# Transposing masked scores on TensorE in the first two chunks of an attention and feed-forward kernel

## The chip, the core and the metric

The kernel runs on one core of one Trainium2 chip, as one program with one launch. The metric is the device time of that program in microseconds. Five engines work side by side: TensorE (PE in the rows, its weight loads PEld), VectorE (DVE), ScalarE (ACT), GpSimd (POOL) and SyncE (SP), whose queue issues nearly all transfers.

## What is computed

The reference is sliding-window attention with four sink keys, followed by a two-layer feed-forward with an ELU between (B = 4, H = 8, S = 768, D = 64, 3072 tokens, d_model = 512, d_ff = 2048, all float32):

```
scores = q @ k.T / sqrt(D)
keep = (key < n_sink) | ((0 <= row - key) & (row - key < window))
scores = where(keep, scores, -1e9) - max
a = exp(scores);  a = a / (sum(a) + 1e-9)
x = a @ v                                  # heads side by side: 3072 x 512
h = x @ w_in;  g = h if h > 0 else exp(h) - 1
out = g @ w_out
```

## The kernel before

The 3072 tokens are cut into ten chunks of two or three tiles of 128 rows (`CHUNKS`). Chunks 0 and 1 take the first tile of each of the four sequences: there all keys of a query lie in one tile, so one 128x128 block of scores per head and tile is enough. They go through `attention_f32`, the others through `attention`. For each chunk attention is done for four pairs of heads (`NP`), and `feed_forward` follows: for each of 16 blocks of d_ff (`NF`), `stage1` forms h (line 867), ACT, DVE and POOL form ELU split into two float16 halves, and `stage2` adds g @ w_out into PSUM (line 897). The feed-forward of chunks 0 and 1 is cut in halves of eight blocks that alternate (`PARTS`), while the 32 pieces of the weights are still being loaded and converted. A piece goes from its load (`raw`) through an ACT step into the one PSUM bank (line 338), bit steps on POOL, ACT or DVE (lines 339 to 343), a DVE step (line 344), and two halves on ACT (line 503) and POOL (line 504).

In `attention_f32` one pair of heads goes through these steps:

- `scores` (line 593): queries times keys, query rows on partitions, two heads, for each of two tiles.
- line 600, DVE: one instruction scales by -0.125, adds the mask, writes the result to a tile `e` and takes its minimum along the row into `tops` (a second, short instruction reads the minimum out).
- `turned` (lines 607 to 610): the scores are computed a second time with keys on partitions (line 607), the mask is added by a matmul with an identity (line 609) and the row's minimum by another with eight times the identity (line 610).
- line 615, ACT: exp, out of PSUM into `pt`.
- `values` (line 631): values times `pt`, with the 64 columns of a head on partitions, and a matmul with a tile of ones which leaves the sum in every one of 64 rows.
- lines 640 to 645: the sum scaled (ACT or DVE), its reciprocal over 128x256 elements (DVE, line 641), the product (DVE, line 642), and two float16 halves (ACT, line 644; DVE or POOL, line 645). Their tile `x` is the input of `stage1`.

Chunk 0 alternates between two pairs of PSUM banks (`s` and `acc`) and three for the products; chunk 1 has one pair (`s`) and one bank (`last_end`).

The order of the work comes from a planner (`Plan`). Every step is a `Task` with an engine, a duration in the planner's terms, dependencies and ring buffers. The planner places the tasks, tries some 250 variations and keeps the best; `keep_order` then fixes the order of the instructions on each engine and of the transfers on SP. So a step that waits holds up all that stands behind it on its engine. `filled` puts matmuls that compute nothing (line 1242) in front of early PE tasks where the planner sees a gap. The first transfers stand ahead of the plan (line 1267).

Of the kernel before, what the change touches and what calls it, by code (L numbers as in the profile page):

```python
# [20 lines left out]
P = 128  # L21
# [29 lines left out]
TURNED = 2  # L51
# [9 lines left out]

KQ_OFF, V_OFF, KQ_COLS, V_COLS = {}, {}, 0, 0
for _c, _ch in enumerate(CHUNKS):
    for _p in range(NP):
        V_OFF[_c, _p] = V_COLS
        V_COLS += (len(key_tiles(_ch)) + 1) * P
        for _e in range(2):
            KQ_OFF[_c, 2 * _p + _e] = KQ_COLS
            if _c >= WHOLE or _e:
                KQ_COLS += len(key_tiles(_ch)) * KW + len(_ch) * P  # L70
# [9 lines left out]
class Task:  # L80
    __slots__ = ("eng", "dur", "lat", "fn", "args", "deps", "succ", "pos", "start", "due", "n", "ways", "done", "gap", "port", "mode", "turn")

    def __init__(self, eng, dur, fn, args, deps, lat, pos, gap, port, mode):
# [14 lines left out]
class Plan:  # L98
# [17 lines left out]
    def add(self, eng, dur, fn, *args, deps=(), lat=0.0, pos=None, or_=(), gap=2.0, port=None, mode=None):  # L116

        t = Task(eng, dur, fn, args, deps, lat, pos, gap, port, mode)
        for way in or_:
            t.ways[way[0]] = way[1:]  # L120
        self.tasks.append(t)
        return t
# [55 lines left out]
    def replay(self, dice=None):  # L178
# [7 lines left out]
        ready = dict.fromkeys(self.tasks, 0.0)  # L186
# [49 lines left out]
    def forward(self):  # L236
        left = {t: len(t.deps) for t in self.tasks}
        ready = {t: 0.0 for t in self.tasks}
# [156 lines left out]
def fast_path(tc, ctx, first, kq, vx, wt, out, nw, inside, flag, limits):  # L395
# [45 lines left out]
    ident8 = pool.tile([P, P], F16, name="ident8")  # L441
    ident16 = pool.tile([P, P], BF16, name="ident16")
    nc.scalar.activation(ident16, ident, AF.Copy)
    nc.scalar.activation(ident8, ident, AF.Copy, scale=8.0)
# [115 lines left out]
    def attention_f32(c):  # L560
# [6 lines left out]
        kw, vw = kc + qc, nt * P  # L567
# [3 lines left out]
        for p in range(NP):  # L571
# [14 lines left out]
            for j in range(nt):  # L586
# [8 lines left out]
                sc = add("PE", 0.25 if c or k > 2 else 0.55, scores, mode="rows", deps=[ldk], pos=at[k])  # L595
# [717 lines left out]
```

## Time and profile before

| what | us |
|---|---|
| median of 3 runs | 628.2 |
| lowest, highest | 626.99, 628.41 |
| the profiled execution, its own time | 628.24 |
| its span, first to last instruction | 626.2 |
| PE busy | 610.9 (98%) |
| DVE busy | 489.3 (78%) |
| ACT busy | 443.4 (71%) |
| POOL busy | 270.5 (43%) |

The span is 2.0 us shorter than the execution's own time. The busy shares are means over the whole span; PE's ends are modelled, so its busy time is an upper figure. The feed-forward lines 867 and 897 hold most of PE's time (1920 and 1200 matmuls).

### The profile page before, as it was taken

Reading aid. Unit: us, or ns where it says so; the run is one execution under the profiler, and the core shown is the slowest. Engines: PE = TensorE matmul, PEld = TensorE weight load, DVE = VectorE, ACT = ScalarE, POOL = GpSimd, SP = SyncE. Lnnn points to the kernel's source line nnn. Section 1 sums busy time; section 2 is a strip of 40 time slices with the busy share of each in tenths; the row PEclk is TensorE's granted clock in tenths of the full one; section 3 lists DMA queues with packets and bytes.
Section 4 is the critical chain, followed back from the end, with each engine's and each line's share of the span. In section 5 each row is a group of like instructions: output and inputs, shape, how many; then the busy total and the mean of one; then the engine's idle time right before and its main releaser. Section 6 shows DMA issues by size and latency. Waiting matters only on the chain.

```text
span 626.2 us, 14317 instructions
## 1 busy us (share of the span) xinstructions
PE 610.9 (98%) x4861; PEld 388.7 (62%) x4861; DVE 489.3 (78%) x1309; ACT 443.4 (71%) x1263; POOL 270.5 (43%) x531
## 2 busy tenths in 40 slices
PE   8899899999999999999999999999999999999997
PEld 6666566667776555667755556766455567765553
DVE  4988889999987567899997689998986899732222
ACT  2478999998887467699875578887765788733222
POOL 2557778555543343445342344433434445412221
PEclk9899999999999999999999999999999999999999
DMA  8467487779986455698974867987937688700001
GB/s 314 130 233 270 128 257 277 185 194 248 210 172 169 109 143 122 146 246 189 169 207 91 211 128 191 204 193 163 231 88 180 138 223 161 162 19 35 1 0 57
DMA packets 127427, 103.18 MB, mean 165 GB/s; under 512 B 96498, under 2 KB 102898, under 8 KB 127346
## 3 DMA queue, kind: packets, MB, share of 16 engines
q1 hardware_dynamic: 127200, 102.12, 65.9%
q8 instruction: 40, 0.66, 0.4%
q14 instruction: 41, 0.34, 0.2%
q10 hardware_dynamic: 146, 0.07, 0.0%
HBM read 71.75 MB, written 7.34 MB: 126 GB/s over the span
## 4 chain that ended last, share of the span: by engine, by line
PE 83%; DVE 6%; ACT 6%; issue 2%; DMA 1%; POOL 0%; SPq 0%; ACTq 0%; DVEq 0%; POOLq 0%
PE h L867 35%; PE acc L897 28%; PE last_acc L897 6%; PE s L756 2%; PE s L757 2%; PE last_end L827 2%; PE s L827 2%; DMA kqs<-in_kq_dram 1%; DVE rx L641 1%; ACT last_acc L338 1%; ACT w L503 1%; PE last_end L631 1%; ACT g L875 1%; DVE wv L344 1%; ACT gh L881 1%
## 5 line engine op out<-in xcount | busy, mean ns | idle before, releaser
L867 PE MATMUL h<-x,w 128*128 128x256 f16 (+1 forms) x1920 | 275.5, 294 | 3.7 <-DVE gl L883 1.5
L867 PEld LDWEIGHTS <-w 128*128 128x128 f16 x1920 | 187.0, 98 | 78.9 <-issue 5.0
L886 POOL TENSOR_TENSOR gl<-g,gh 128x256 f16<-128x256 f32 (+1 forms) x143 | 118.4, 829 | 189.2 <-ACT gh L881 145.9
L897 PE MATMUL acc<-w,gh 128*128 128x512 f16 x636 | 175.0, 379 | 0.0
L897 PEld LDWEIGHTS <-gh 128*128 128x128 f16 x792 | 74.7, 98 | 67.3 <-ACT gh L881 0.6
L875 ACT ACTIVATE g<-h 128x256 f32<-128x256 f32 (+1 forms) x160 | 67.1, 420 | 62.4 <-PE h L867 57.8
L881 ACT ACTIVATE gh<-g 128x256 f16<-128x256 f32 (+1 forms) x143 | 65.7, 460 | 50.0 <-DVE g L880 49.3
L897 PE MATMUL acc<-w,gl 128*128 128x512 f16 x318 | 96.9, 379 | 0.1
L781 ACT ACTIVATE e<-e,st 128x264 f32<-128x264 f32 x160 | 81.5, 510 | 18.2 <-DVE st L779 17.7
L794 DVE SCALAR_TENSOR_TENSOR pq<-e,st,pq 128x256 f16<-128x256 f32 x160 | 84.4, 548 | 7.9 <-ACT pq L793 7.4
L877 DVE TENSOR_SCALAR g<-g 128x256 f32<-128x256 f32 (+1 forms) x95 | 34.6, 364 | 71.1 <-ACT g L875 70.5
L793 ACT ACTIVATE pq<-e,st 128x256 f16<-128x256 f32 x160 | 75.4, 503 | 6.8 <-ACT g L875 3.2
L880 DVE SCALAR_TENSOR_TENSOR g<-g,h 128x256 f32<-128x256 f32 (+1 forms) x144 | 68.3, 475 | 6.5 <-ACT g L877 5.1
L779 DVE CUSTOM_DVE_ANT_0 e<-s,m 128x264 f32<-128x264 f32 x160 | 64.6, 426 | 6.4 <-PE s L757 5.7
L897 PEld LDWEIGHTS <-gl 128*128 128x128 f16 x396 | 38.1, 98 | 44.5 <-DVE gl L883 0.5
L682 ACT ACTIVATE kq<-kqs 128x912 f16<-128x912 f32 (+1 forms) x56 | 48.0, 862 | 8.5 <-PE s L757 5.4
L785 POOL TENSOR_SCALAR st<-st 128x2 f32<-128x2 f32 x80 | 21.5, 269 | 70.3 <-ACT e L781 60.0
L897 PE MATMUL last_acc<-w,gh 128*128 128x512 f16 (+1 forms) x126 | 45.3, 366 | 0.0
L504 POOL TENSOR_TENSOR w<-wv,w 128x512 f16<-128x512 f32 x32 | 39.0, 1226 | 13.8 <-ACT w L503 13.5
L685 DVE SCALAR_TENSOR_TENSOR kq<-kqs,kq 128x528 f16<-128x528 f32 (+1 forms) x56 | 38.0, 679 | 2.7 <-ACT kq L682 1.9
L756 PE MATMUL s<-kq 128*128 128x264 f16 x144 | 37.2, 276 | 0.2 <-DVE st L779 0.2
L757 PE MATMUL s<-kq 128*128 128x264 f16 x144 | 37.2, 276 | 0.0
(170 smaller groups left out, 837.9 us busy)
## 6 DMA issues: line engine op xcount, KB each, us to landing
raw<-in_wt_dram SPq DMA_DIRECT2D x32, 512.0 KB, 4.8
kqs<-in_kq_dram SPq DMA_DIRECT2D x32, 456.0 KB, 3.9
kqs<-in_kq_dram SPq DMA_DIRECT2D x28, 326.0 KB, 3.4
out_dram<-wv SPq DMA_DIRECT2D x21, 256.0 KB, 4.4
vs<-in_vx_dram SPq DMA_DIRECT2D x16, 320.0 KB, 4.2
qk<-in_kq_dram SPq DMA_DIRECT2D x24, 195.0 KB, 5.2
vs<-in_vx_dram SPq DMA_DIRECT2D x16, 256.0 KB, 3.3
qk<-in_kq_dram SPq DMA_DIRECT2D x24, 163.0 KB, 4.2
```

The lines of the kernel that those rows point to most:

```text
L756: nc.tensor.matmul(sp[:, :wd], q, hi[:, c0 : c0 + wd], start=True, stop=False)
L757: nc.tensor.matmul(sp[:, :wd], q, lo[:, c0 : c0 + wd], start=False, stop=True)
L779: red = add("DVE", 0.08 + 0.00104 * wd, lambda ee=ee, me=me, sp=sps[e], m=m, wd=wd: nc.vector.tensor_tensor_reduce(ee, sp[:, :wd], m[:, :w ...
L781: ex = add("ACT", act_us(wd, sums=True), lambda ee=ee, me=me, rs=rs[:, e : e + 1]: nc.scalar.activation(ee, ee, AF.Exp, bias=me, scale=-1. ...
L793: a = add("ACT", act_us(nb * P, True), lambda src=src, hi=hi, re=re: nc.scalar.activation(hi, src, AF.Copy, scale=re), deps=[rr])
L794: b = add("DVE", dve_us(nb * P) + 0.03, lambda src=src, hi=hi, lo=lo, re=re: nc.vector.scalar_tensor_tensor(lo, src, re, hi, ALU.mult, ALU ...
L867: nc.tensor.matmul(hp[:, :n], win[:, part, d, :], xx[:, :n], start=k == 0, stop=k == 3 * ND - 1)
L875: a = add("ACT", act_us(n) + 0.06, lambda gf=gf, hp=hp, sums=sums: nc.scalar.activation(gf, hp[:, :n], AF.Exp, scale=1.0 / G_SCALE, accum_ ...
L880: b = add("DVE", dve_us(n) - 0.035, lambda gf=gf, gd=gd, hp=hp: nc.vector.scalar_tensor_tensor(gd, gf, 0.0, hp[:, :n], ALU.min, ALU.max), ...
L881: th = add("ACT", act_us(n) - (0.03 if near else 0.0), lambda gd=gd, gh=gh: nc.scalar.activation(gh[:, :n], gd, AF.Copy), deps=[b])
L886: tl = add("POOL", pool_us(n), lambda gl=gl, gd=gd, gh=gh: nc.gpsimd.tensor_tensor(gl[:, :n], gd, gh[:, :n], ALU.subtract), deps=[th])
L897: nc.tensor.matmul(to[:, : cols.stop - cols.start], gg[:, i * P : (i + 1) * P], wout[:, part, cols], start=f == f0 and k == 0, stop=f == f ...
```

## The change

- In `attention_f32`, `turned` no longer computes the scores again. It transposes the masked scores `e` that DVE has written, in TensorE's transpose mode, two per task, and takes the minimum off by a matmul with minus the identity (`minus`). The matmul that added the mask is gone, and exp's scale becomes -1.
- `values` has `pt` as the stationary operand: queries are rows, and there are 65 columns for each head and tile. The 65th column of the values, which the layout of the input now carries, is a constant, so that the sum comes out beside the product. There are four matmuls in the place of eight.
- The sum's constant is added, and its reciprocal taken, on 128x4 elements, both on DVE. The product is formed with that column broadcast. A new step `upright` turns the product back by two TensorE transposes into the same bank; ACT and DVE make the float16 halves out of PSUM (POOL has no such step any more).
- The ring `e` is now given back by `turned` rather than by the DVE step; `kqs` is given back by the scores alone; the bank of the product is given back by the last of the float16 halves.
- The first transfers are issued in another order (both `kqs` ahead of `vs`), and the planner gets earliest times (`floor`, `LANDED`) for two PE tasks, filler matmuls up to 20.0 of its own time rather than 9.0, and two other durations on POOL.

The diff, cut to its core:

```diff
         V_OFF[_c, _p] = V_COLS
-        V_COLS += (len(key_tiles(_ch)) + 1) * P
+        V_COLS += 2 * len(_ch) * (D + 1) if _c < TURNED else (len(key_tiles(_ch)) + 1) * P
...
-    ident8 = pool.tile([P, P], F16, name="ident8")
-    ident16 = pool.tile([P, P], BF16, name="ident16")
-    nc.scalar.activation(ident16, ident, AF.Copy)
-    nc.scalar.activation(ident8, ident, AF.Copy, scale=8.0)
+    minus = pool.tile([P, P], F16, name="minus")
+    nc.scalar.activation(minus, ident, AF.Copy, scale=-1.0)
...
-                sc = add("PE", 0.25 if c or k > 2 else 0.55, scores, mode="rows", deps=[ldk], pos=at[k])
+                sc = add("PE", 0.25 if c or k > 2 else 0.55, scores, mode="rows", deps=[ldk], pos=at[k], floor=0.0 if c or p != 1 else LANDED[0])
...
-                def turned(sps=sps, st=st, keys=keys, qs=qs, tr=tr, mn=mn, j=j):
+                def turned(sps=sps, e3=e3, to=to, tr=tr, mn=mn, j=j):
                     for e in range(2):
-                        r = slice(e * D, (e + 1) * D)
-                        nc.tensor.matmul(sps[e][:, tr], st[r, keys], st[r, qs], start=True, stop=False)
+                        nc.tensor.matmul(sps[e][:, tr], e3[:, e, to], ident, is_transpose=True, start=True, stop=False)
                     for e in range(2):
-                        nc.tensor.matmul(sps[e][:, tr], m0[:, NS:KW], ident16, start=False, stop=False)
-                        nc.tensor.matmul(sps[e][:, tr], mn[:, 2 * e + j : 2 * e + j + 1].to_broadcast([P, P]), ident8, start=False, stop=True)
-
-                tn = add("PE", 0.45 if c or k > 2 else 0.8, turned, mode="turned", deps=now, pos=at[k] + 1.5)
+                        nc.tensor.matmul(sps[e][:, tr], mn[:, 2 * e + j : 2 * e + j + 1].to_broadcast([P, P]), minus, start=False, stop=True)
+
+                tn = add("PE", 0.37 if c or k > 2 else 0.75, turned, mode=None, deps=now, pos=at[k] + 1.5)
                 turns.append(tn)
                 k += 1
-            exps = [add("ACT", act_us(qc), lambda pt=pt[:, e * qc : (e + 1) * qc], sp=sps[e][:, qc : 2 * qc]: nc.scalar.activation(pt, sp, AF.Exp, scale=0.125), deps=turns) for e in range(2)]
+            exps = [add("ACT", act_us(qc), lambda pt=pt[:, e * qc : (e + 1) * qc], sp=sps[e][:, qc : 2 * qc]: nc.scalar.activation(pt, sp, AF.Exp, scale=-1.0), deps=turns) for e in range(2)]
...
-            ring("e", reds, reds)
+            ring("e", reds, turns)
             if held:
-                ring("kqs", [ldk or scored[0]], scored + turns)
+                ring("kqs", [ldk or scored[0]], scored)
...
             po = (*po_ps, *h_ps)[out_bank]
+            rows3 = po[:, :vw].rearrange("p (g w) -> p g w", w=D + 1)
 
             def values(po=po, vr=vr, pt=pt):
                 for j in range(nt):
-                    for sums in range(2):
-                        oc = slice(sums * qc + j * P, sums * qc + (j + 1) * P)
-                        for e in range(2):
-                            vv = first["ones_d"] if sums else vr[:, j * P + e * D : j * P + (e + 1) * D]
-                            nc.tensor.matmul(po[e * D : (e + 1) * D, oc], vv, pt[:, e * qc + j * P : e * qc + (j + 1) * P], start=j + sums == 0, stop=j == nt - 1 and sums == 1)
-
-            val = add("PE", 0.03 + 0.216 * 2 * nt, values, mode="columns", deps=[ldv, *exps], pos=at[k - 1] + 4.0)
+                    for e in range(2):
+                        oc = slice((2 * j + e) * (D + 1), (2 * j + e + 1) * (D + 1))
+                        nc.tensor.matmul(po[:, oc], pt[:, e * qc + j * P : e * qc + (j + 1) * P], vr[:, oc], start=True, stop=True)
+
+            val = add("PE", 0.7, values, deps=[ldv, *exps], pos=at[k - 1] + 4.0, floor=0.0 if c or p else LANDED[1])
...
             rx = rxs[slot("rx")]
+            rs = sts[slot("st")][:, 0 : 2 * nt]
             xh, xl = x_room(qc)
-            xf = po[:, qc : 2 * qc]
-            a = add("ACT", act_us(qc) - 0.03, lambda rx=rx, xf=xf: nc.scalar.activation(rx, xf, AF.Copy, scale=1.0 / X_SCALE, bias=1.0e-9 / X_SCALE), deps=[val], or_=[("DVE", dve_us(qc) - 0.03, lambda rx=rx, xf=xf: nc.vector.tensor_scalar(rx, xf, 1.0 / X_SCALE, 1.0e-9 / X_SCALE, ALU.mult, ALU.add))])
-            b = add("DVE", dve_us(qc), lambda rx=rx: nc.vector.reciprocal(rx, rx), deps=[a])
-            b = add("DVE", dve_us(qc) - 0.03, lambda rx=rx, po=po: nc.vector.tensor_tensor(rx, po[:, :qc], rx, ALU.mult), deps=[b])
-            ring(f"po{out_bank or ''}", [val], [b])
-            fa = add("ACT", act_us(qc), lambda xh=xh, rx=rx: nc.scalar.activation(xh, rx, AF.Copy), deps=[b])
-            fb = add("DVE", dve_us(qc), lambda xh=xh, xl=xl, rx=rx: nc.vector.tensor_tensor(xl, rx, xh, ALU.subtract), deps=[fa], port=True, or_=[("POOL", pool_us(qc), lambda xh=xh, xl=xl, rx=rx: nc.gpsimd.tensor_tensor(xl, rx, xh, ALU.subtract))])
-            ring("rx", [a], [fa, fb])
+            a = add("DVE", 0.1, lambda rs=rs, rows3=rows3: nc.vector.tensor_scalar(rs, rows3[:, :, D], 1.0e-9 / X_SCALE, None, ALU.add), deps=[val])
+            a = add("DVE", 0.1, lambda rs=rs: nc.vector.reciprocal(rs, rs), deps=[a])
+            b = add("DVE", dve_us(qc) - 0.03, lambda rx=rx, rs=rs, rows3=rows3: nc.vector.tensor_tensor(rx.rearrange("p (g w) -> p g w", w=D), rows3[:, :, :D], rs.unsqueeze(2).to_broadcast([P, 2 * nt, D]), ALU.mult), deps=[a])
+            ring("st", [a], [b])
+
+            def upright(po=po, rx=rx):
+                for j in range(nt):
+                    nc.tensor.transpose(po[:, j * P : (j + 1) * P], rx[:, j * P : (j + 1) * P], ident)
+
+            up = add("PE", 0.24, upright, deps=[b], pos=at[k - 1] + 7.0)
+            ring("rx", [b], [up])
+            fa = add("ACT", act_us(qc) - 0.03, lambda xh=xh, po=po: nc.scalar.activation(xh, po[:, :qc], AF.Copy), deps=[up])
+            fb = add("DVE", dve_us(qc) - 0.03, lambda xh=xh, xl=xl, po=po: nc.vector.tensor_tensor(xl, po[:, :qc], xh, ALU.subtract), deps=[fa])
+            ring(f"po{out_bank or ''}", [val], [fa, fb])
...
-    pe[0].fn = filled(pe[0].fn, first["warm"], h_ps[1], 1)
+    pe[0].fn = filled(pe[0].fn, first["warm"], po_ps[0], 1)
     for a, b in zip(pe, pe[1:]):
-        b.fn = filled(b.fn, first["warm"], h_ps[1] if b.start < 9.0 else acc[2], int((b.start - a.start - a.dur - 0.1) / 0.11 + (b.start < WARM_BY)))
+        gap = b.start - a.start - a.dur
+        b.fn = filled(b.fn, first["warm"], po_ps[0], int((gap - 0.1) / 0.11 + (b.start < WARM_BY and gap > 0.05)))
...
-WARM_BY, WARM_UNTIL = 8.0, 9.0
+WARM_BY, WARM_UNTIL = 8.0, 20.0
+LANDED = 5.3, 6.0
...
+            w = D + 1 if c < TURNED else D
+            o = V_OFF[c, h // 2] + e * w
             for g in kts:
                 vx[:, o : o + D] = v[g // NT, h, g % NT * P : (g % NT + 1) * P]
-                o += P
+                if c < TURNED:
+                    vx[:, o + D] = 1.0 / X_SCALE
+                o += 2 * w
...
             ("kqs", 0, kq, KQ_OFF[0, 0], nk * KW + qc),
-            ("vs", 0, vx, V_OFF[0, 0], (nk + 1) * P),
             ("kqs", 1, kq, KQ_OFF[0, 2], nk * KW + qc),
+            ("vs", 0, vx, V_OFF[0, 0], 2 * nk * (D + 1)),
```

The planner's order is new from end to end. Three places are shown, as each engine's queue holds them.

PE, from the first pair's scores on (`kqs_81` is the first pair's input, `kqs_82` the second's, whose transfer comes later; const-bfloat16 rows are fillers). Before:

```order
L593 MATMUL s_186<-kqs_81 128x128
L593 MATMUL s_187<-kqs_81 128x128
L593 MATMUL acc_93<-kqs_82 128x128
L593 MATMUL acc_94<-kqs_82 128x128
L607 MATMUL s_186<-kqs_81 128x128
L607 MATMUL s_187<-kqs_81 128x128
L609 LDWEIGHTS m_188
```

Now:

```order
L592 MATMUL s_186<-kqs_81 128x128
L592 MATMUL s_187<-kqs_81 128x128
L1251 LDWEIGHTS const-bfloat16-1.0
L1251 MATMUL last_end<-const-bfloat16-1.0 128x248
L605 MATMUL s_186<-ident,e_109 128x128
L605 MATMUL s_187<-ident,e_109 128x128
L607 LDWEIGHTS tops
```

The second pair's scores stood between the first pair's scores and its turned scores; they now stand behind both turned tasks of the first pair.

DVE, from a product of chunk 0 in bank `h_184` to its float16 half (ISA rows are line 600 or 599, `wv` rows are the weights' line 344 or 345). Before:

```order
L640 TENSOR_SCALAR rx_143<-h_184 128x256
L600 ISA e_109,tops<-acc_94,m_188 128x128
L600 ISA tops 128x1
L641 RECIPROCAL rx_143<-rx_143 128x256
L344 SCALAR_TENSOR_TENSOR wv_138<-last_acc,wu_144 128x512
L642 TENSOR_TENSOR rx_143<-h_184,rx_143 128x256
L371 TENSOR_SCALAR m_190<-sv_137 128x128 x2
```

Now:

```order
L636 TENSOR_SCALAR st_113<-h_184 128x4
L599 ISA e_109,tops<-acc_94,m_188 128x128
L599 ISA tops 128x1
L637 RECIPROCAL st_113<-st_113 128x4
L599 ISA e_109,tops<-acc_94,m_188 128x128
L599 ISA tops 128x1
L638 TENSOR_TENSOR rx_143<-h_184,st_113 128x256
L345 SCALAR_TENSOR_TENSOR wv_138<-last_acc,wu_144 128x512
```

The reciprocal of 256 columns is one of 4, and the weights' step that stood between it and the product now stands behind the product.

PE, from the last product of chunk 0 (in `last_end`, from `sv_136`) to the next pair's scores (`upright` is line 643 and has no counterpart before; before, the rows behind a product were the next scores or turned scores, and nothing of it came back to PE but `x`). Now:

```order
L627 MATMUL last_end<-sv_136,pt_124 128x65 x4
L605 MATMUL s_186<-ident,e_110 128x128
L605 MATMUL s_187<-ident,e_110 128x128
L607 LDWEIGHTS tops
L607 MATMUL s_186<-minus,tops 128x128
L607 LDWEIGHTS tops
L607 MATMUL s_187<-minus,tops 128x128
L643 MATMUL h_185<-ident,rx_142 128x128 x2
L592 MATMUL s_186<-kqs_82 128x128
```

The product's own `upright` stands further down: behind a turned task, the `upright` of the pair before (`h_185`), two score tasks and five fillers, and ahead of the turned scores of the third pair of chunk 1 and the first `stage1`.

## Rows read from the trace of the kernel before

**Rows 1.** Windows, five stretches: us; busy PE, PEld, DVE, ACT, POOL; PEclk, DMA, GB/s.

```profile
0.00:8.50 8.50, 6.51 (x37) 4.54 (x38) 4.06 (x25) 1.79 (x3) 2.02 (x20) 1.00 0.76 251
8.50:32.50 24.00, 20.83 (x194) 15.55 (x193) 19.15 (x68) 11.23 (x27) 10.31 (x13) 0.87 0.59 204
32.50:66.40 33.90, 30.51 (x247) 19.49 (x245) 29.90 (x69) 27.68 (x73) 23.25 (x25) 0.99 0.74 261
66.40:112.00 45.60, 44.71 (x342) 28.95 (x341) 40.24 (x94) 44.03 (x124) 35.27 (x47) 1.00 0.69 210
112.00:600.00 488.00, 486.54 (x3916) 308.10 (x3915) 388.27 (x1031) 351.80 (x1022) 195.09 (x424) 1.00 0.69 157
```

**Rows 2.** Chain of waits, 8 to 34 us, shares by line.

```profile
by line: DVE rx L641 19.5%; PE last_end L631 17.0%; PE s L607 10.4%; DVE e L600 8.2%; PE h L867 5.3%; DVE m L371 5.0%; PE s L593 4.6%; PE s L609 4.6%; DVE wv L344 4.1%; PE s L610 2.9%; PE acc L593 2.8%; PE acc L607 2.8%; DVE rx L640 2.6%; D
```

**Rows 3.** Timeline of PE: start, us, instruction, idle before it and releaser.

```profile
6.02 0.80 PE L593 MATMUL acc<-kqs 64*128 64x128 f32 x4 [1.22 <-DMA kqs<-in_kq_dram]
25.17 0.70 PE L607 MATMUL s<-kqs 64*128 64x128 f32 x4 [2.19 <-DVE tops L600]
32.52 1.80 PE L867 MATMUL h<-x,w 128*128 128x256 f16 x12
```

**Rows 4.** Windows of PE alone: us, busy, granted clock, DMA, GB/s.

```profile
27.00:33.00 6.00, 5.53 (x38) 0.50 0.48 156
34.00:40.00 6.00, 5.85 (x61) 1.00 0.64 216
```

**Rows 5.** DVE and POOL steps by line (ns min/median/max), and line 641 from 8 to 34 us.

```profile
L641 DVE RECIPROCAL rx<-rx x8: 1741/1748/1753, 13.4 to 60.1; 128x256 f32<-128x256 f32 x8
8.00:34.00 26.00, 8.74 (x5) 0.87 0.59 205
L786 DVE RECIPROCAL st<-st x80: 140/160/169, 67.4 to 543.3; 128x2 f32<-128x2 f32 x80
L375 DVE TENSOR_SCALAR sv<-sv,words x1: 223/223/223, 3.8 to 3.8; 128x4 f32<-128x4 f32 x1
L642 DVE TENSOR_TENSOR rx<-last_end,rx x6: 409/414/420, 15.8 to 62.7; 128x256 f32<-128x256 f32 x6
L645 POOL TENSOR_TENSOR x<-rx,x x5: 672/673/863, 16.8 to 59.5; 128x256 f16<-128x256 f32 x5
```

**Rows 6.** Timeline of PE, the steps of attention (starts show the pitch).

```profile
3.58 1.23 PE L593 MATMUL s<-kqs 64*128 64x128 f32 x8
...
8.99 0.80 PE L607 MATMUL acc<-kqs 64*128 64x128 f32 x4
...
12.83 0.49 PE L607 MATMUL acc<-kqs 64*128 64x128 f32 x4
...
13.58 0.71 PE L593 MATMUL s<-vm 64*128 64x128 f32 x8
14.21 0.71 PE L593 MATMUL acc<-vm 64*128 64x128 f32 x6
...
15.60 0.44 PE L631 MATMUL h<-pt,vs 128*64 128x128 f32 x4
...
16.63 0.49 PE L607 MATMUL s<-vm 64*128 64x128 f32 x4
17.05 0.23 PE L609 MATMUL s<-ident,m 128*128 128x128 bf16 x1
17.12 0.22 PE L610 MATMUL s<-ident,tops 128*128 128x128 f16 x1
17.17 0.22 PE L609 MATMUL s<-ident,m 128*128 128x128 bf16 x1
...
17.38 0.49 PE L607 MATMUL s<-vm 64*128 64x128 f32 x4
```

**Rows 7.** Timeline of ACT: exp of the first and the eighth block of feed-forward.

```profile
34.36 0.38 ACT L875 ACTIVATE g<-h 128x256 f32<-128x256 f32 x1 [1.29 <-PE h L867]
...
66.42 0.36 ACT L875 ACTIVATE g<-h 128x256 f32<-128x256 f32 x1
```

More of the change, by code (lines that the diff above doesn't have):

```diff
@@ L50 @@
 WHOLE = 3
-TURNED = 2
 AHEAD = 5
@@ L59, in key_tiles @@
     return sorted({g for g in ch} | {g - 1 for g in ch if g % NT})
+TURNED = 2
 KQ_OFF, V_OFF, KQ_COLS, V_COLS = {}, {}, 0, 0
@@ L80, with __init__ @@
 class Task:
-    __slots__ = ("eng", "dur", "lat", "fn", "args", "deps", "succ", "pos", "start", "due", "n", "ways", "done", "gap", "port", "mode", "turn")
-    def __init__(self, eng, dur, fn, args, deps, lat, pos, gap, port, mode):
+    __slots__ = ("eng", "dur", "lat", "fn", "args", "deps", "succ", "pos", "start", "due", "n", "ways", "done", "gap", "port", "mode", "turn", "floor")
+    def __init__(self, eng, dur, fn, args, deps, lat, pos, gap, port, mode, floor):
+        self.floor = floor
         self.gap, self.port, self.mode = gap, port, mode
@@ L114, in __init__, with add @@
         self.tasks, self.rings = [], {}
-    def add(self, eng, dur, fn, *args, deps=(), lat=0.0, pos=None, or_=(), gap=2.0, port=None, mode=None):
-        t = Task(eng, dur, fn, args, deps, lat, pos, gap, port, mode)
+    def add(self, eng, dur, fn, *args, deps=(), lat=0.0, pos=None, or_=(), gap=2.0, port=None, mode=None, floor=0.0):
+        t = Task(eng, dur, fn, args, deps, lat, pos, gap, port, mode, floor)
         for way in or_:
@@ L185, in replay @@
         left = {t: len(t.deps) for t in self.tasks}
-        ready = dict.fromkeys(self.tasks, 0.0)
+        ready = {t: t.floor for t in self.tasks}
         free, dma, lock, mode, last = dict(self.BEGIN), self.LOADED, 0.0, None, 0.0
@@ L237, in forward @@
         left = {t: len(t.deps) for t in self.tasks}
-        ready = {t: 0.0 for t in self.tasks}
+        ready = {t: t.floor for t in self.tasks}
         later = {e: [] for e in self.HOP}
@@ L566, in attention_f32 @@
         kc, qc = nt * KW, nt * P
-        kw, vw = kc + qc, nt * P
+        kw, vw = kc + qc, 2 * nt * (D + 1)
         at = times(c)
@@ L729, in attention @@
             if far:
-                vb = add("POOL", 0.35, lambda vhi=vhi, vlo=vlo: nc.gpsimd.tensor_copy(vhi[64:72, nk * P :], vlo[64:72, nk * P :]), deps=[vb], port=False)
+                vb = add("POOL", 0.5, lambda vhi=vhi, vlo=vlo: nc.gpsimd.tensor_copy(vhi[64:72, nk * P :], vlo[64:72, nk * P :]), deps=[vb], port=False)
             ring("vhl", [va], v_users)
@@ L804, in sinks @@
                         nc.gpsimd.tensor_tensor(hi[:, 1, :], flat, hi[:, 0, :], ALU.subtract)
-                    b = add("POOL", 0.92, sinks, deps=[rr], port=False)
+                    b = add("POOL", 1.12, sinks, deps=[rr], port=False)
                     parts.append(b)
@@ L956, in fast_path @@
         kts = key_tiles(ch)
-        o, wd, at = V_OFF[c, 0], (len(kts) + 1) * P, kts.index(ch[0]) * P
+        o, wd, at = V_OFF[c, 0], V_OFF[c, 1] - V_OFF[c, 0], kts.index(ch[0]) * P
+        n = wd if c < TURNED else n
         src = vx[:, o : o + NP * wd].rearrange("p (a w) -> p a w", a=NP)[:, :, at : at + n]
@@ L1119, in general_path @@
                     nc.sync.dma_start(qt[:, ts], kq[r, o : o + P])
-                    o = V_OFF[c, h // 2] + j * P + (h % 2) * D
+                    o = V_OFF[c, h // 2] + ((2 * j + h % 2) * (D + 1) if c < TURNED else j * P + (h % 2) * D)
                     nc.sync.dma_start(vt[:, g % NT, :], vx[:, o : o + D])
@@ L1199, in layouts @@
                     o += w
-            o = V_OFF[c, h // 2] + e * D
+            w = D + 1 if c < TURNED else D
+            o = V_OFF[c, h // 2] + e * w
             for g in kts:
                 vx[:, o : o + D] = v[g // NT, h, g % NT * P : (g % NT + 1) * P]
-                o += P
+                if c < TURNED:
+                    vx[:, o + D] = 1.0 / X_SCALE
+                o += 2 * w
             if far:
@@ L1258, in attention_moe @@
         first = {n: [pool.tile([P, w], F32, name=f"{n}{i}") for i in range(RINGS[n])] for n, w in widths.items()}
-        first["spread"], first["warm"], first["ones_d"] = spread, warm, nc.const_aps.tensor(1.0, [P, D], F32)
+        first["spread"], first["warm"] = spread, warm
         first["kq"], first["vs_"] = {(0, 0), (0, 2)}, {(0, 0)}
```

## Prediction

> **What bounds the kernel now.** I first cut the span into stretches of the windows view, to see where PE has time left [rows 1]. From 112 to 600 us it is busy 486.54 of 488.00 us, and from 66.4 to 112 us 44.71 of 45.60: whatever comes earlier to 112 us is handed on to the end, since the change touches nothing behind it but the order. What can be won lies ahead of 66.4 us. Of the 24 us from 8.5 to 32.5 the chain of waits gives most to one DVE line: the reciprocal of line 641 with 19.5%, ahead of any PE line [rows 2]. It takes 1.75 us each, eight times, five of them begun between 8 and 34 us, the last at 60.1 [rows 5]. DVE is busy 19.15 of the 24 us there, ACT only 11.23 [rows 1]. The timeline of PE has the consequences: 1.22 us idle for a transfer of the second pair's keys, 2.19 us idle for DVE before 25.17, and the first `stage1` only at 32.52 [rows 3]. After that idle time TensorE's granted clock is 0.50 of full from 27 to 33 us, its level of 1.2 GHz, and 1.00 (2.4 GHz) from 34 us on [rows 4]. In the first stretch the clock row reads 1.00, but durations say otherwise: eight instructions of the scores took 1.23 us at 3.58 and moved on after 0.63 us at 13.58 [rows 6]. I go by durations there and call the first price slow, the second full.
>
> The profiled execution took 628.24 us beside a median of 628.2, so the sum below is made against 628.24 and carried over as it is.
>
> **DVE.** Gone: eight reciprocals, 8 x 1.75 = 14.0 us. In their place eight additions and eight reciprocals on 128x4. The trace has none of just these; the nearest rows are a 128x4 step of 0.22 us and a 128x2 reciprocal of 0.16 us [rows 5], so 8 x 0.38 = 3.0 us (at the least half of it, at the most twice). Line 645 goes to DVE in all eight cases; five were on POOL at 0.67 us [rows 5], and the 256-column DVE step costs 0.41 us [rows 5]: +2.1 us. Line 640 had four of its eight on DVE, which go: I leave those about 1.7 us against it uncounted and call the relief 9 us. Up to the fourth half of `x`, which the first `stage1` needs, four reciprocals go: 19.15 - 4 x 1.75 + 4 x 0.38 + 2 x 0.41 = 14.5 us of DVE work from 8.5 us on, so DVE allows the first `stage1` from about 23 us.
>
> **PE's attention steps.** A turned task runs 0.75 us, from 16.63 to 17.38 at the full price [rows 6]. Its four-row f32 matmul pair takes 0.42 of it (16.63 to 17.05), a 128-column matmul in 16 bits 0.055 (17.12 to 17.17) [rows 6]. Now it is two transposes and two of the small matmuls. The trace shows no transpose on TensorE. Lower bound: like a 16-bit matmul, 0.055. Upper bound: like the f32 matmul, 0.21. I take 0.11, half of that, one pass in place of two, so 2 x 0.11 + 2 x 0.055 and a lead of 0.05 make 0.37 us (0.27 to 0.60). `values` runs from 15.60 to 16.63, 1.03 us, in 16 instructions with 64 columns to load [rows 6]; now eight with 128 to load and 65 to move, between half, 0.5, and 1.03 us. I take 0.8. `upright` is two transposes, 0.2 us. Per pair: before 2 x 0.75 + 1.03 = 2.5, now 2 x 0.37 + 0.8 + 0.2 = 1.75.
>
> By the Trainium skill (TensorE: Matmul & The Clock Gate, Part 4: PE-mode transpose) a 128x128 transpose of bf16 took about 0.275 us inside a kernel. No run here shows it yet. With it the 48 transposes would cost about 13 us in place of 5, an estimate from that page, and the time would be near 626 if nothing hid them.
>
> **When the first stage1 starts.** In the new order 12 score tasks, 12 turned tasks, four `values` and four `upright` stand between the first pair's scores and the first `stage1`. At the full price: 12 x 0.32 (from 0.63 for two at 13.58 [rows 6]) + 12 x 0.37 + 4 x 0.8 + 4 x 0.2 + fillers 0.7 = 13 us. They can begin at about 5.5: the scores are out at 4.8 and DVE's minimum follows, and the wait for the second pair's transfer is no longer in front of the turned scores. Before, the slow price held to about 12.8 us (four instructions of line 607 took 0.80 us at 8.99 and 0.49 at 12.83 [rows 6]); if it does so again, that adds some 3.7 us. So PE allows about 22, DVE about 23. I add 1 us for waits between the two and take 24. Against 32.5 to 32.7 that is **8.7 us earlier**.
>
> **From the first to the eighth block.** Exp of the first block runs at 34.36, of the eighth at 66.42 [rows 7], 32 us, in which PE idles 33.90 - 30.51 = 3.4 us [rows 1]. PE's own work there changes little: fewer turned tasks are left, but four `values` and four `upright`. DVE loses the last three reciprocals, 5.2 of 29.90 us [rows 1, 5], and the weights, whose DVE step stood behind them, come sooner. PE can win at most its 3.4 us and perhaps 1 of work; I take **2.5**.
>
> **After 66.4 us** PE idles 0.9 us to 112 and 1.5 us to 600 [rows 1], so nothing is to be won. But the order is new throughout, ACT is busy 44.03 of 45.60 us to 112 [rows 1], and its work now has to fit behind an earlier start. I take **1 us lost** (0 to 3).
>
> Costing nothing: the longer hold of the ring `e` (three buffers, DVE has a slack of a pair), the earlier return of `kqs` (its loads wait for less), the moved first transfer (`vs` is needed only after exp, some 3 us after the scores), the layout's 65th column (1040 bytes a row in place of 1024). The POOL steps that go were off the chain. If the cover of `vs` failed, PE would idle as it now does for `kqs`, 1.2 us.
>
> **Sum:** 628.2 - 8.7 - 2.5 + 1.0 = **618.0 us**.
>
> **Rivals.**
>
> 1. *TensorE stays at its slow level until the first stage1.* The new stream has less for PE to do between the same waits, and the trace shows what follows idle time: 0.50 granted from 27 to 33 us, after 2.19 us idle [rows 3, 4]. The 13 us then cost some 1.9 times (1.23 against 0.63) [rows 6], about 25 us from 5.5 on: the first `stage1` at 31, only 1.7 us sooner. With 2.5 and no other loss the time is 624. Against it: the gaps of 1.22 and 2.19 us that precede slow stretches are the ones that go, and fillers stand in the new gaps. Chance 0.21. The same page of the Trainium skill says that a transpose in this mode does not bring the array to its full clock, which would favour this rival; the trace of before has no such transpose and cannot show it.
> 2. *The product's way back makes PE wait (slower).* Each of the eight `upright` needs the product's addition, reciprocal and multiplication from a DVE queue that is busy 88% of 32.5 to 66.4 us [rows 1], and all feed-forward behind it on PE waits too. Where a weights step or two stands ahead on DVE, such a wait is 1 to 1.5 us. Eight of 1.5 us are 12 us: 618 + 12 = 630. It decides above 1.3 us each, since 8 x 1.3 is the gain. Against it: in the order shown several PE tasks stand between a product and its `upright`. Chance 0.07.
> 3. *The weights keep their old pace.* If load and conversion of the weights, not DVE's reciprocals, set the blocks from 34 to 66 us, an earlier start is given back and step eight still comes near 66: 627.5. For it: 27.68 of 33.90 us on ACT. Against it: ACT idles over half of 8.5 to 32.5 us, and DVE, on which the weights' steps wait, is what gets free. Chance 0.05.
> 4. *PE never waits.* The first `stage1` at 21.5, all 3.4 us won, nothing lost later: 628.2 - 11 - 3.4 = 613.5. Chance 0.07.
>
> The forecast itself, 614 to 622, has 0.60.
>
> **Range and chances.** The unknown prices move the sum little alone: transposes at 0.055 or 0.21 make about -2 or +5 us in PE's sum, `values` -1 or +1. From 613 to 626 the range holds the forecast, most of rival 1 and half of rival 4. A measurement of this kernel tells 0.2%, 1.3 us, from no change. Faster: 0.60 + 0.21 + 0.07 = 0.88; same: rival 3, 0.05; slower: rival 2, 0.07.
>
> **What would show it.** Right: line 637 at 0.15 to 0.2 us; the first `stage1` at 22 to 26 us; exp of the eighth block near 55; 112 to 600 us as full as now. Wrong: a granted clock of 0.50 or slow durations past 13 us (rival 1); PE idle in front of line 643 with DVE as the releaser (rival 2); a first `stage1` at 24 us but an eighth block near 66 (rival 3).

## The result and the profile after

The changed kernel takes 620.66 us (median of 4 runs, 619.07 to 621.79) beside 628.31 us for the kernel before (median of 4 runs): a ratio of 0.9878, 95% interval 0.9846 to 0.9909, or 7.65 us less. The forecast was 618.0 in a range of 613 to 626. The profiled execution took 619.07 us, its span is 616.7 us against 626.2.

The windows of the changed kernel, in the stretches of [rows 1] (columns as there):

```profile
8.50:32.50 24.00, 21.67 (x182) 18.20 (x181) 19.72 (x94) 15.94 (x39) 11.80 (x13) 1.00 0.77 277
32.50:66.40 33.90, 32.57 (x227) 21.93 (x226) 30.46 (x84) 31.62 (x86) 24.80 (x30) 1.00 0.82 279
66.40:112.00 45.60, 43.62 (x330) 27.74 (x329) 41.66 (x96) 42.62 (x119) 31.94 (x45) 1.00 0.73 213
112.00:600.00 488.00, 488.00 (x3923) 308.74 (x3922) 384.92 (x1023) 344.88 (x1000) 188.60 (x415) 1.00 0.66 153
```

The gain lies ahead of 66.4 us. From there to 112 us PE idles 1.1 us more than before (busy 43.62 against 44.71 us), and behind that it is full. DVE is as busy from 8.5 to 32.5 us as before (19.72 against 19.15 us), but with 94 instructions in place of 68: where long reciprocals stood there are now steps of the work that follows. ACT got 4.7 us more done there, and the granted clock is 1.00 instead of 0.87.

PE's timeline, the answer to [rows 3, 6] (start, duration, instruction, idle time before it and releaser):

```profile
11.98 1.23 PE L592 MATMUL s<-vm 64*128 64x128 f32 x8
13.00 0.90 PE L592 MATMUL acc<-vm 64*128 64x128 f32 x8
13.83 1.11 PE L627 MATMUL h<-vs,pt 128*128 128x65 f32 x8
14.77 0.39 PE L643 MATMUL last_end<-ident,rx 128*128 128x128 f32 x2
15.00 0.38 PE L605 MATMUL s<-ident,e 128*128 128x128 f32 x2
15.21 0.28 PE L607 MATMUL s<-minus,tops 128*128 128x128 f16 x2
15.33 0.39 PE L605 MATMUL s<-ident,e 128*128 128x128 f32 x2
...
25.36 1.48 PE L870 MATMUL h<-x,w 128*128 128x256 f16 x12
...
30.48 0.44 PE L643 MATMUL last_end<-ident,rx 128*128 128x128 f32 x2 [0.82 <-DVE rx L638]
```

The steps follow one another from start to start, which gives their prices: `values` 0.94 us (13.83 to 14.77), `upright` 0.23, two transposes 0.21 and a whole turned task 0.33 (15.00 to 15.33). The first `stage1` starts at 25.36 us, against 32.52. TensorE moves on after 1.02 us for eight score instructions at 11.98 and after 0.83 at 13.00: the full price begins inside the latter, and it stays.

The DVE steps, by line (ns min/median/max, first and last start), which answer to [rows 5]:

```profile
L637 DVE RECIPROCAL st<-st x8: 161/168/173, 11.5 to 52.9; 128x4 f32<-128x4 f32 x8
L638 DVE TENSOR_TENSOR rx<-last_end,st x6: 405/416/419, 13.6 to 53.3; 128x256 f32<-128x256 f32 x6
```

And exp of the first and of the eighth block, for [rows 7]:

```profile
26.98 0.38 ACT L878 ACTIVATE g<-h 128x256 f32<-128x256 f32 x1
...
56.61 0.39 ACT L878 ACTIVATE g<-h 128x256 f32<-128x256 f32 x1
```

The lead is 7.4 us at the first block (34.36 to 26.98) and 9.8 us at the eighth (66.42 to 56.61). The same line gives 9.6 us at block 24 and 9.5 at block 32, where the two spans also end apart.

Where the chain of waits still leaves PE, between 5 and 25 us (start, us, what):

```profile
15.95 0.60 DVE wv L345
16.55 0.33 DVE x L648
16.88 1.29 DVE m L372 x3
18.17 0.13 DVE e L599
...
21.98 0.04 issue
22.02 0.70 PE last_end L1251 x5
```

No reciprocal is among its large pieces any more. Three mask steps of the later chunks (line 372, 1.29 us), which nothing near needs, stand ahead of the minima, and five fillers take 0.70 us on the path itself.

### The profile page after: what moved, and what is told of

It is laid out like the page before. It is cut to its first block, busy times and chain, and to the rows that moved or that the text cites. A ratio compares the mean times of both kernels' runs of the same rounds, so it can differ in the third digit from the quotient of the medians.

```text
span 616.7 us, 14108 instructions
## 1 busy us (share of the span) xinstructions
PE 604.2 (98%) x4757; PEld 387.5 (63%) x4757; DVE 484.6 (79%) x1324; ACT 441.5 (72%) x1253; POOL 262.4 (43%) x525
## 3 DMA queue, kind: packets, MB, share of 16 engines
q1 hardware_dynamic: 127200, 102.09, 66.4%
## 4 chain that ended last, share of the span: by engine, by line
PE 88%; ACT 5%; DVE 4%; issue 1%; POOL 0%; DMA 0%; DVEq 0%; ACTq 0%
PE h L870 37%; PE acc L900 31%; PE last_acc L900 6%; PE s L759 3%; PE s L760 3%; PE last_end L830 2%; PE s L830 2%; DVE wv L345 1%; ACT last_acc L339 1%; ACT w L502 1%; PE s L592 1%; DVE wu L343 1%; PE last_end L627 1%; ACT g L878 1%; ACT gh L884 0%
## 5 line engine op out<-in xcount | busy, mean ns | idle before, releaser
L889 POOL TENSOR_TENSOR gl<-g,gh 128x256 f16<-128x256 f32 (+1 forms) x143 | 117.1, 819 | 179.5 <-ACT gh L884 141.3
L880 DVE TENSOR_SCALAR g<-g 128x256 f32<-128x256 f32 (+1 forms) x103 | 37.2, 361 | 70.4 <-ACT g L878 69.8
```

What stands on the lines that cost most here:

```text
L889: tl = add("POOL", pool_us(n), lambda gl=gl, gd=gd, gh=gh: nc.gpsimd.tensor_tensor(gl[:, :n], gd, gh[:, :n], ALU.subtract), deps=[th])
```

## Experiments

The theory was that DVE's wide reciprocals held back the first `stage1`, and that the new turned scores are cheaper as costed. Its rivals: that the gain is the changed preparations' (load order, floors, fillers), or the work that left PE, or TensorE's clock. All variants compute the whole result. "First stage1" and "exp 8" are the starts, in each variant's profiled execution, of the two steps named above.

| kernel | median us (range, runs) | ratio to before, 95% | first stage1 | exp 8 |
|---|---|---|---|---|
| changed_again | 620.47 (619.65 to 622.22, 5) | 0.9858 to 0.9899 | 25.16 | 56.89 |
| wide_reciprocal | 633.38 (632.81 to 634.12, 4) | 1.0065 to 1.0099 | 32.37 | 69.46 |
| no_values_change | 627.35 (625.88 to 629.47, 10) | 0.9961 to 0.9994 | 31.49 | 68.15 |
| no_turned_change | 635.24 (632.47 to 636.04, 4) | 1.0070 to 1.0118 | 39.78 | 72.66 |
| no_turned_dense | 625.48 (624.76 to 625.89, 4) | 0.9923 to 0.9965 | 31.39 | 62.45 |
| no_setup_change | 618.91 (617.30 to 619.66, 4) | 0.9823 to 0.9858 | 27.49 | 58.95 |
| no_fillers | 621.29 (619.81 to 622.44, 5) | 0.9859 to 0.9899 | 26.23 | 58.72 |
| late_masks | 618.69 (616.56 to 623.06, 6) | 0.9820 to 0.9878 | 29.58 | 59.94 |
| late_masks_no_fillers | 616.22 (615.10 to 621.88, 6) | 0.9789 to 0.9857 | 23.70 | 54.26 |
| late_fill | 618.69 (616.25 to 621.62, 6) | 0.9809 to 0.9864 | 27.45 | 57.05 |
| late_masks_old_setup | 616.01 (613.09 to 618.04, 6) | 0.9764 to 0.9827 | 22.46 | 54.47 |

### The reciprocal alone, as wide as before

The order of all instructions is that of the changed kernel; only the reciprocal is taken of the broadcast column (the product then reads that result as it lies).

```diff
-            a = add("DVE", 0.1, lambda rs=rs: nc.vector.reciprocal(rs, rs), deps=[a])
+            a = add("DVE", 0.1, lambda rs=rs: nc.vector.reciprocal(wide_r.rearrange("p (g w) -> p g w", w=D), rs.unsqueeze(2).to_broadcast([P, 2 * nt, D])), deps=[a])
```

> The changed kernel with the reciprocal of line 637 taken again over 128x256 elements (the sum broadcast, result in a buffer of its own), eight times, in exactly the order of the changed kernel. Theory (DVE's long reciprocals held the way to the first stage1): eight times 1.6 us more on DVE, of which DVE's idle time between 8.5 and 23.5 us (3.2 us) can hide a part, so the first stage1 at 29 to 32 us in place of 25.4, and 5 to 9 us above the changed kernel: near 627. Rival (the shorter PE steps made the gain, DVE follows): 0 to 2 us above it, near 621 to 622.

Its line 638, its windows, and its waits of PE up to 80 us (waiting instruction and releaser: us in total, times, longest):

```profile
L638 DVE RECIPROCAL wide_r<-st x8: 1739/1744/1747, 11.3 to 64.8; 128x256 f32<-128x256 f32 x8
```

```profile
23.50:32.50 9.00, 6.37 (x37) 4.67 (x38) 6.01 (x21) 4.42 (x9) 3.70 (x5) 0.63 0.58 205
32.50:66.40 33.90, 28.38 (x192) 19.62 (x192) 29.83 (x73) 25.13 (x66) 19.22 (x21) 0.95 0.64 212
```

```profile
PE last_end L644 <- DVE rx L639: 3.1, 3, 1.8
PE last_end L1252 <- DVE rx L639: 1.7, 1, 1.7
PE last_end L628 <- DVE x L649: 1.7, 2, 0.8
PE s L606 <- DVE tops L600: 1.4, 2, 1.1
```

Eight steps 1.58 us longer each (12.6 us in all) cost 12.9 us against changed_again, more than the 5 to 9 expected, and the first `stage1` falls back by 7.2 us. So the variant loses the whole gain, but not by DVE's time alone. PE's timeline of this kernel, then of changed_again, whose instructions on PE are the same:

```profile
12.80 1.06 PE L593 MATMUL acc<-vm 64*128 64x128 f32 x8
...
19.09 0.39 PE L644 MATMUL h<-ident,rx 128*128 128x128 f32 x2
...
27.33 1.19 PE L1252 MATMUL last_end<-const-bfloat16-1.0 128*128 128x248 bf16 x5 [1.69 <-DVE rx L639]
...
32.37 2.74 PE L871 MATMUL h<-x,w 128*128 128x256 f16 x12
...
36.29 1.47 PE L871 MATMUL h<-x,w 128*128 128x256 f16 x12
...
40.22 0.44 PE L644 MATMUL last_end<-ident,rx 128*128 128x128 f32 x2 [1.78 <-DVE rx L639]
```

```profile
12.81 0.78 PE L592 MATMUL acc<-vm 64*128 64x128 f32 x8
...
16.10 0.39 PE L643 MATMUL h<-ident,rx 128*128 128x128 f32 x2
...
21.83 0.70 PE L1251 MATMUL last_end<-const-bfloat16-1.0 128*128 128x248 bf16 x5
...
25.16 1.48 PE L870 MATMUL h<-x,w 128*128 128x256 f16 x12
...
27.32 1.47 PE L870 MATMUL h<-x,w 128*128 128x256 f16 x12
...
30.28 0.44 PE L643 MATMUL last_end<-ident,rx 128*128 128x128 f32 x2 [0.82 <-DVE rx L638]
```

Up to 12.8 us the two run alike. There changed_again turns to the full price, and this kernel stays slow until some 18.9 us. At the `upright` on `h` it is 3.0 us behind (19.09 against 16.10), with only 0.36 us of a wait for DVE. The granted clock falls after the waits, to 0.63 from 23.5 to 32.5 us, and the slow price lasts until about 36. Of the 9.9 us by which the last row lags, some 6.1 are stretches at the slow price (2.6 up to 19.09, 1.7 from 27.33 to 32.37, 1.8 from there to 36.29) and 3.8 are waits, an estimate from these starts and the idle times between them. The fall follows waits for DVE; no row shows that DVE delayed the turn. What the wide reciprocal costs at an even clock was not measured.

In this variant the prediction's second rival comes true as well: PE waits 3.1 us for `upright` (line 644 here) and 1.7 us more in the fillers ahead of one. In the changed kernel one `upright` waited, 0.82 us.

### The product's part undone

The old `values` with the tile of ones, and the wide sum and reciprocal, with the new turned scores. The planner made its own order for it.

```diff
-                    for e in range(2):
-                        oc = slice((2 * j + e) * (D + 1), (2 * j + e + 1) * (D + 1))
-                        nc.tensor.matmul(po[:, oc], pt[:, e * qc + j * P : e * qc + (j + 1) * P], vr[:, oc], start=True, stop=True)
+                    for sums in range(2):
...
+                            nc.tensor.matmul(po[e * D : (e + 1) * D, oc], vv, pt[:, e * qc + j * P : e * qc + (j + 1) * P], start=j + sums == 0, stop=j == nt - 1 and sums == 1)
```

> The changed kernel with the old product of values, the old sum in 64 rows and the old reciprocal over 128x256, newly planned; the transposed scores stay. Theory: the reciprocals are back, so 5 to 8 us above the changed kernel, 625.5 to 628. Rival: 0 to 3 us above it, 620 to 623.

PE's timeline before its first `stage1` (line 864 here):

```profile
27.03 2.23 PE L1241 MATMUL last_end<-const-bfloat16-1.0 128*128 128x248 bf16 x10 [4.01 <-DVE rx L639]
...
31.49 1.47 PE L864 MATMUL h<-x,w 128*128 128x256 f16 x12
```

PE stands still for 4.01 us in front of the last pair, for the product behind DVE's reciprocal. Behind the wait ten fillers take another 2.2 us, and the granted clock is 0.58 from 27 to 31 us. The kernel is worth 1 us against before and lies 6.9 above changed_again, as expected: with the wide reciprocals in place, what the cheaper turned scores save mostly goes into waits and fillers.

### The turned scores undone

The old second computation of the scores, with the mask's matmul, beside the new product, in an order of its own by the planner.

```diff
-                        nc.tensor.matmul(sps[e][:, tr], e3[:, e, to], ident, is_transpose=True, start=True, stop=False)
+                        nc.tensor.matmul(sps[e][:, tr], st[r, keys], st[r, qs], start=True, stop=False)
...
-                        nc.tensor.matmul(sps[e][:, tr], mn[:, 2 * e + j : 2 * e + j + 1].to_broadcast([P, P]), minus, start=False, stop=True)
+                        nc.tensor.matmul(sps[e][:, tr], m0[:, NS:KW], ident16, start=False, stop=False)
+                        nc.tensor.matmul(sps[e][:, tr], mn[:, 2 * e + j : 2 * e + j + 1].to_broadcast([P, P]), ident8, start=False, stop=True)
```

> The changed kernel with the old turned scores (computed a second time, mask and minimum added by matmuls), newly planned. Theory (reciprocals make most of the gain): PE has 16 x 0.35 = 5.6 us more work ahead of 40 us, about half of it beside waits: 2 to 4 us above the changed kernel, 622 to 625. Rival (the transposed scores make most of the gain): 6 to 8 us above, no different from the kernel before.

PE in its timeline, then its windows:

```profile
33.22 0.80 PE L608 MATMUL s<-kqs 64*128 64x128 f32 x4
...
39.78 2.77 PE L874 MATMUL h<-x,w 128*128 128x256 f16 x12
...
43.84 1.36 PE L874 MATMUL h<-x,w 128*128 128x256 f16 x11
```

```profile
8.50:23.50 15.00, 14.06 (x82) 10.62 (x79) 6.06 (x43) 2.33 (x6) 2.82 (x4) 1.00 0.65 233
23.50:32.50 9.00, 8.96 (x51) 7.48 (x49) 4.70 (x21) 4.38 (x11) 2.95 (x3) 1.00 0.16 61
```

This is 14.8 us slower than changed_again, which neither expectation had, and slower than the kernel before, although DVE is busy for only 10.76 of the 24 us from 8.5 to 32.5. PE is busy 23.02 of these 24 us, but at the slow price: four score instructions take 0.80 us still at 33.22, and twelve of `stage1` 2.77 us at 39.78 against 1.47 at the full price. It is the first rival's case. The clock row reads 1.00 all the same; durations have to be read again. Only the reason differs from the rival's: PE hardly idles here.

To separate price from work, the same kernel was run with 16 filler matmuls in one block at 8.5 us, same order:

```diff
+    pe[4].fn = filled(pe[4].fn, first["warm"], po_ps[0], 16)
```

> The kernel with the old turned scores from above (635.2 us; PE busy nearly throughout, at slow durations until 42 us), with one edit: 16 filler matmuls in one block in front of the second pair's scores, near 8.6 us; order otherwise the same. They cost 16 x 0.21 = 3.3 us at the slow price. Theory (TensorE's slow durations, not the amount of work, made that kernel slower than before): durations turn fast at or soon after the block, by 20 us at the latest, the first stage1 comes at 28 to 32 us in place of 39.8, and the time falls to 624 to 629. Rival (PE's work in the old turned scores costs that much by itself): the block only adds, 636 to 639.

```profile
8.49 3.41 PE L1256 MATMUL last_end<-const-bfloat16-1.0 128*128 128x248 bf16 x16
11.83 0.72 PE L594 MATMUL acc<-kqs 64*128 64x128 f32 x8
...
31.39 1.47 PE L874 MATMUL h<-x,w 128*128 128x256 f16 x12
```

Adding 3.3 us of useless work (8.49 to 11.83 in this timeline) makes the kernel 9.8 us faster: the full price holds from 11.83 us on and the first `stage1` comes 8.4 us sooner. So most of what undoing the turned scores costs is TensorE's clock. The other 5.0 us (625.48 against 620.47) hold the old turned scores' work, the block itself and the other order, which were not told apart.

### The preparations

Old load order, no floors, fillers as before:

```diff
-WARM_BY, WARM_UNTIL = 8.0, 20.0
-LANDED = 5.3, 6.0
+WARM_BY, WARM_UNTIL = 8.0, 9.0
+LANDED = 0.0, 0.0
```

(The second `kqs` goes back behind `vs` in the list of first transfers.)

> The changed kernel with the first transfers in the old order, no earliest times for the planner (both 0) and fillers only up to 9.0 of the planner's time. Theory (they only keep PE from waiting about 1.2 us for the second pair's keys): 0.5 to 2 us above the changed kernel, about 622. Rival (TensorE's clock stays at its slow level without them): slow durations past 13 us, 3 us or more above it, 624 or more.

618.91 us: its interval ends where that of changed_again begins (0.9858). So the preparations are no part of the gain, and may cost some 1.5 us, where 0.5 to 2 us of worth had been expected. Its profiled execution kept the slow price until some 18.5 us, and `stage1` came 2.3 us later than in changed_again, at 27.49 us; its span still ends 0.5 us sooner (617.6 against 618.1), for a reason that was not followed up.

Without any planned filler, in the same order:

```diff
-    pe[0].fn = filled(pe[0].fn, first["warm"], po_ps[0], 1)
-    for a, b in zip(pe, pe[1:]):
-        gap = b.start - a.start - a.dur
-        b.fn = filled(b.fn, first["warm"], po_ps[0], int((gap - 0.1) / 0.11 + (b.start < WARM_BY and gap > 0.05)))
```

> The changed kernel without any of the nine planned fillers, order otherwise the same. Theory (fillers only cost): the one in front of the first product and the five in front of an upright stand on the chain with 0.3 and 0.55 us; without them 0.3 to 0.9 us below the changed kernel. Rival (they hold the clock): TensorE's durations stay slow past 13 us or fall again, the first stage1 comes later than 26 us, 1 to 4 us above it.

Timeline and one window:

```profile
23.73 1.01 PE L592 MATMUL s<-kqs 64*128 64x128 f32 x4 [0.34 <-DVE tops L599]
...
26.23 2.74 PE L870 MATMUL h<-x,w 128*128 128x256 f16 x12
```

```profile
23.50:32.50 9.00, 8.77 (x52) 7.15 (x52) 5.13 (x23) 5.19 (x14) 4.23 (x4) 0.62 0.64 218
```

The clock fell after the waits for `tops`, to 0.62 in this stretch, and `stage1` took 2.74 us. The time is the same within the intervals, so neither what the fillers cost nor what they win shows in it.

The changed kernel once more:

> The changed kernel itself, unaltered, for the comparison with the three beside it: 619 to 622 us. If the first run's spread comes from when TensorE turns fast, the turn shows at another time than 12.8 us in this profile and the time moves with it; if it does not, the turn is at the same time or the time does not follow.

The first `stage1` came at 25.16 us and the full price at 12.8, against 25.36 and 13.0 in the first profile, and yet the span is 1.4 us longer (618.1 against 616.7). Between these two executions it is not the turn that differs. What makes the spread of 2.6 us stays open.

### The masks on the chain

The three mask steps get an earliest time, so that the planner places them later:

```diff
-    rest_ = add("DVE", 0.7, mask2, deps=[mask1_])
+    rest_ = add("DVE", 0.7, mask2, deps=[mask1_], floor=32.0)
```

> The changed kernel with the planner told that the third mask (three DVE steps of line 372, 1.3 us from 16.8 us on, on the chain of waits there) may not be placed before 32 us. Theory (these steps stood in the way of the first stage1): it comes 0.5 to 1.3 us earlier, and the time falls by as much. Rival (PE's own work sets the first stage1 once DVE is free): no change within 0.4 us, or the new order costs more than it brings.

618.69 us. In its profiled execution (620.79 us) PE kept the slow price until 25.6 us and the first `stage1` came at 29.58, 4.4 us later than in changed_again and not earlier, so the step's own worth can't be read from it. With the planned fillers gone as well:

> Both edits together. If each takes a wait from the chain: 1 to 2 us below the changed kernel, 618.5 to 619.5. If PE's work sets the first stage1: no lower than the better of the two alone.

616.22 us, lower than the 618.5 to 619.5 expected, and the first `stage1` at 23.70. With late masks, and fillers only between 14 and 40 us of the planner's time:

```diff
-        b.fn = filled(b.fn, first["warm"], po_ps[0], int((gap - 0.1) / 0.11 + (b.start < WARM_BY and gap > 0.05)))
+        b.fn = filled(b.fn, first["warm"], po_ps[0], int((gap - 0.1) / 0.11) if b.start > WARM_BY and gap > 0.1 else 0)
...
-WARM_BY, WARM_UNTIL = 8.0, 20.0
+WARM_BY, WARM_UNTIL = 14.0, 40.0
```

> The changed kernel with the third mask placed late, no fillers before 14 us and fillers in every gap that the planner sees from 14 to 40 of its time. Theory (without fillers the durations fell back to slow once, near 31 us, and cost about 1.5 us): the fall does not come, 614 to 616. Rival (fillers cost as much as they hold): 616 to 618, no lower than without any.

618.69 us, above both expectations: the slow price held until some 19 us, after which the clock did not fall again. Whether the 2.5 us against the version without fillers are the fillers' cost or the later turn isn't told apart: the intervals overlap.

Late masks with the old preparations (the edits of late_masks and no_setup_change together):

> The changed kernel with the third mask placed late, and the transfers, earliest times and fillers as in the run without the change's preparations (618.9 us). If the two gains add: 616 to 617.5. If the order or the moment at which TensorE turns fast decides: anywhere from 615 to 622, with the first stage1 following that moment.

```profile
5.96 0.80 PE L592 MATMUL acc<-kqs 64*128 64x128 f32 x4 [1.17 <-DMA kqs<-in_kq_dram]
...
9.54 1.21 PE L627 MATMUL last_end<-vs,pt 128*128 128x65 f32 x8
10.58 0.39 PE L605 MATMUL acc<-ident,e 128*128 128x128 f32 x2
...
22.46 1.48 PE L870 MATMUL h<-x,w 128*128 128x256 f16 x12
```

At 616.01 us this is the lowest median, its interval (0.9764 to 0.9827) wholly below that of changed_again, but not told apart from late_masks_no_fillers (0.9789 to 0.9857). It touches that of no_setup_change (0.9823 to 0.9858), so the late masks' own share, 2.9 us by the medians, is not shown. The old wait of 1.17 us for `kqs` is back, yet the full price begins at about 10 us and the first `stage1` at 22.46. Three executions lie at 613.1 to 614.2 us, three at 617.9 to 618.0; what parts them is not known.

## Why the prediction was right, and where its sizes were off

**DVE.** The prices are shown: the reciprocal takes 0.17 us in place of 1.75, the addition 0.16, the product 0.42, as taken. Putting the wide reciprocal back, in the same order, took back more than the gain, through waits for DVE and through the slow price together. That DVE's time alone carried the first `stage1` is argued, not shown.

**PE's prices.** Turned 0.33 us (taken 0.37), the transpose 0.11 (taken 0.11), `upright` 0.23 (taken 0.2), `values` 0.94 at 13.83 and 0.84 at 26.68, where the next step starts at 27.52 (taken 0.8, in bounds of 0.5 and 1.03). The sum per pair is 1.73 to 1.83 us against the 1.75 taken. The 0.275 us of the Trainium skill (TensorE: Matmul & The Clock Gate, Part 4: PE-mode transpose), there for bf16, is near one instruction's own duration here (0.28 us for a single f32 transpose at 22.64 in wide_reciprocal), but not the price: successive ones start 0.105 us apart, and the time near 626 that went with it did not come. The other rule of the same page of the Trainium skill, that a transpose does not bring the array to its full clock, is neither borne out nor refuted. From 14.77 to 16.66 us PE ran `upright` and turned tasks alone and stayed at the full price, and the variant that stayed slow past 42 us has no turned transposes (only those of `upright`); but variants with them stayed slow to 18.5, 18.9, 19 and 25.6 us, and between the transposes stand ordinary small matmuls.

**First `stage1`.** Taken 24, measured 25.36 and 25.16: the earlier start is worth 7.2 us, not 8.7. The step that is off is "fillers 0.7" and "1 us for waits": the chain from 5 to 25 us gives the fillers' line 1251 7.8%, 1.6 us, and three mask steps 1.29 us, which the prediction had not looked for. The slow price held to 13.0 us, as it was taken to, but that is luck as far as the runs show: with the same instructions on PE up to 12.8 us it lasted to 18.9 in wide_reciprocal. Part of the lead is TensorE's clock, which the sum did not name as a term. Before, PE was busy 5.53 us at 0.50 from 27 to 33 us [rows 4]; at the full price that is about half, so some 2.8 us by this estimate, and the changed kernel's clock did not fall there (1.00 from 8.5 to 32.5 us).

**Up to the eighth block.** Taken 2.5 us, measured 32.06 - 29.63 = 2.4. PE's idle time from 32.5 to 66.4 us fell from 3.4 to 1.3.

**After 66.4 us.** Taken 1 us lost. PE's idle time from there to 112 us rose from 0.9 to 2.0, and the lead went from 9.8 us to 9.5 at block 32 (with 11.3 at the sixteenth between). In the profiled executions the sum is thus -7.4 - 2.4 + 0.3 = -9.5 by the exps, which the spans repeat; the own times differ by 9.2 (628.24 to 619.07) and the medians by 7.65, because the profiled execution was the shortest of its kernel's four. So of the 2.7 us between forecast and median, 1.4 come from the first `stage1` and 1.6 from the other executions (620.66 less 619.07); the rest nearly cancels.

**Rivals.** The first did not happen in the profiled executions of the changed kernel, but did in no_turned_change, and in part in wide_reciprocal. Its factor of 1.9 sets a duration (1.23) against a time between starts (0.63). Between starts alone eight score instructions take 1.02 us at 11.98, 1.6 times as much, and a turned task 0.64 us at 10.57 against 0.33, which is 1.9. The second happened with the wide reciprocal, where it had not been looked for. The third fell: the blocks came faster. For the fourth, PE would have to wait nowhere, and it idles 2.3 us from 8.5 to 32.5 and 1.3 from there to 66.4 (its own sum comes to 613.8, not 613.5).

## What to carry to other kernels

Divide where the sum is one column, not where it is spread: a DVE step off the busiest engine may still hold the first use of its result, and its price is read where the chain of waits passes through it. When an early stretch is rebuilt, read durations there as well as the granted clock, since the same instructions can run at one price or at nearly twice that. A variant that puts one step back can also differ in when the full price begins, so compare its starts row by row before its loss is put down to the step. Try preparations (load order, fillers, earliest times) apart from the rest: here they earned nothing. With the old preparations, and one step that nobody near needs given a later earliest time, the kernel was 4.5 us faster still, though which of the two did how much was not shown.

## What was not expected of the hardware

- The moment at which TensorE's durations become short lies anywhere from about 10 us (late_masks_old_setup) to past 42 us (no_turned_change). PE's own instructions do not settle it: changed_again and wide_reciprocal have the same on PE, with starts equal to 0.02 us, up to 12.8 us, where one turns and the other stays slow to 18.9. So do late_masks_no_fillers and late_fill up to 13.6 us, where the next `values` takes 1.18 us in one and 1.97 in the other. With one block of 16 matmuls in front, no_turned_dense turned at 11.8 us. What decides it is left open, and a first `stage1` from one profiled execution carries this uncertainty.
- The granted clock reads 1.00 from 8.5 to 42 us of no_turned_change, where scores (0.80 us for four at 33.22) and `stage1` (2.77 us at 39.78) take nearly twice as long as at the full price. Later falls do show in that row: 0.63 in wide_reciprocal and 0.62 in no_fillers, both from 23.5 to 32.5 us.
- A wide step whose input is a broadcast column costs DVE as much as on full data: 1.744 us for the reciprocal over 128x256 from 128x4, 1.748 us before [rows 5].
